# Attention, cosine feed-forward and soft mixture of experts on one core: a weight conversion one tile further ahead, and attention products and a transpose in other slots

## The chip, the core and the metric

One core of one Trainium2 chip runs the kernel. The metric is device time in microseconds (us), the median of three runs. Engines are called as in the profile: PE (matrix products), DVE and POOL (elementwise work), ACT (activations), SP (a queue that issues DMAs).

## The reference

```python
kv = einsum('bhsd,bhse->bhde', k, v);  out = einsum('bhsd,bhde->bhse', q, kv)   # 8 x 8 heads, 576 x 64
x = (out / sqrt(mean(out*out) + 1e-6) * g_norm)        # to 4608 tokens x 512
h = x @ w_in                                           # 512 x 2048
x = (h * cos(h)) @ w_out                               # 2048 x 512
logits = x @ phi                                       # 8 experts x 4 slots
d = softmax of logits over the tokens;  slot_input = d.T @ x
slot_out[e] = relu(slot_input[e] @ w1[e]) @ w2[e]      # 512 x 1024, 1024 x 512
out = (softmax of logits over the slots) @ slot_out
```

## The kernel before, in words

The 4608 tokens are worked in ten blocks j: eight of 512 tokens (0 to 7) and two of 256 (8 and 9, `SMALL` is 8). A block has 16 steps, called slots, one for each 128-column tile f of w_in. In a slot the PE makes `main(j, f)`, 12 products into a PSUM bank called h (L391): w_in is split into a rounded part and a low part, and so is x, and three of the four pairs are multiplied for each of four rows of weights. Then come cos_a (ACT L407 and DVE L410), cos_b (ACT L414) and cos_c (DVE L453, which writes gT and frees the h bank). There are three h banks, so a main can't start until the cos_c of three mains before has run. From block 1's second half on, cos_c is followed by DVE transposes (L460, L472) into `tr`, which DMAs carry to `g`. In blocks 8 and 9 two tiles share one 512-column bank, so that two mains (24 products of 256 columns) go with one cos.

Everything else is put into the slots by tables, and a scheduler isn't used: the order of issue is the order of the code. `at2(j, n, f)` puts a call into slot n of block j, and n of 16 or more means slot n-16 of block j+1. What a slot runs is, from block 2 on: loads, main, side calls (these), cos_a, post, cos_b, cos_c, fin.

For blocks 1 to 9 the attention products of block j's tokens run in block j-1. `att_out(j, t)` makes the products ops for 128 tokens (PE L202), ACT squares them (L211), DVE sums (L213), and POOL raises the sum to the power -0.5 (L216, `ri`). `att_xs` multiplies (DVE L223), `att_xT` transposes on the PE (L241) and copies the rounded part (ACT L245), `att_lo` makes the low part (DVE L254). All of these take a bank of a second ring of four, called at.

The softmax over tokens is a running one. For each block `l_exp` (L573 to L580) makes the exponentials `ld`, `l_T` (PE L594, 64-row transposes `ldT`) turns them to tokens, and DVE copies two halves out of the bank, `d` (L596) and `l_tok` (L604). `slot_acc` (PE L624, `ab`) then adds d.T @ g for the block. The expert stage and the output follow after block 9.

The first 60 us are different. w_in and w_out arrive as 64-bit numbers and are converted in the kernel, tile by tile, in letters of the strings `start`, `one` and `two`: A scales (ACT L301), R shifts (DVE L306), P and L put in the sign and the low bits (DVE L311, L316), H rounds (ACT L322) and S subtracts for the low part (POOL L327). Capital letters are w_in (in `one` and `two` for tile f+2, `LI`), small letters w_out. A token such as A.1 names its tile; m0, f0, r0, b0, c0 are main, the two parts of cos_a, cos_b and cos_c of block 0; s0, p0 and e0 are the side, post and fin calls. Block 1 runs four slots (`L`) behind block 0. `start` also makes block 0's attention; block 1's is in the slots of block 0 that `A[0]` names, one list each for products, multiply, transposes, and low parts.

Of the kernel before, what the change touches and what calls it, by code (L numbers as in the profile page):

```python
# [21 lines left out]
PLAN = dict(  # L22
    ke=(0, 0),
    lp=(0, 0, 0),
    gE=(0, 0),
    co=(3, 4, 4, 5, 6, 7, 7, 8, 9, 10, 10, 11, 12, 12, 13, 13),
    wq=(7, 10, 13, 15),
    l0=(9, 9, 12, 13, 15, 15, 17, 17),
    E=((18, 19, 3, 1), (18, 19, 3, 1)),
    F=((21, 22), (21, 22)),  # L30
    L=4,
    LI=2,
    PI=2,
    start=(
# [3 lines left out]
    ),  # L38
    one='m0 e0 A R f0 P a l0 r0 p0 L r s0 b0 H p c0 S l',
    two='s0 m0 A R m1 a f0 e1 P L l0 f1 r0 r1 s1 l1 p0 r b0 H c0 e0 b1 p c1 l S p1',  # L40
    wm=(3, 5),
    pm=3,
    pa=4,
# [3 lines left out]
    lx=(2, 1),  # L47
    lT=20,
    sa=22,
    A=(((0, 0, 1, 2), (1, 1, 1, 1), (2, 2, 3, 3), (0, 0, 0, 0)),  # L50
       ((9, 10, 11, 12), (0, 0, 0, 0), (11, 12, 13, 14), (0, 0, 0, 0))),
    K=((0, (0, 0, 0, 0)), (1, (1, 3, 5, 7)), (1, (13, 15, 17, 19))),
    KL=(((0, 1), (1, 2), (1, 4), (1, 6)), ((1, 11), (1, 14), (1, 16), (2, 2))),
    ao=(2, 5, 8, 11),
    xs=(1, 1, 1, 1),
    xT=(5, 8, 11, 14),
    lo=(1, 1, 0, 0),
# [7 lines left out]
NB = len(SIZES)  # L65
TT = [n // 128 for n in SIZES]
T0 = [sum(TT[:j]) for j in range(NB)]
NT = sum(TT)
SMALL = SIZES.index(256)
# [3 lines left out]
def tile_linear_attention__ffn_cos__soft_moe(  # L73
# [14 lines left out]
    B, H, D = kv.shape[0], 8, 64  # L88
    NF, KD = w_in.shape[0], w_in.shape[2]
# [31 lines left out]
    sel = const.tile([128, 4, NS], F32, name="sel")  # L121
    A_ = const.tile([128, 576], F32, tag="A", name="A")
    A = A_[:, 0:512]
    m_run = const.tile([128, 1], F32, name="m_run")
# [8 lines left out]
    def at_bank(name):  # L133
        return ps_a.tile([128, 512], F32, tag="at", name=name)
# [5 lines left out]
    q_t, kv_t, vr_t = {}, {}, {}  # L140
    kz = rem_p.tile([128, 2, 512], F32, tag="kr", name="kz")

    def spans(j, t):
        p, r = divmod(T0[j] + t, 9)
        if r == 4:
            return [(0, 64, 2 * p), (64, 64, 2 * p + 1)]
        return [(0, 128, 2 * p + r // 5)]

    def load_q(j, t):
        if j == 0:  # L150
            q_t[j, t] = first["q"][:, t]
        else:
            q_t[j, t] = q_p.tile([128, 4, 128], F32, tag=f"q{(T0[j] + t) % 3}", name="q")
        nc.sync.dma_start(out=q_t[j, t], in_=qT[T0[j] + t])
# [22 lines left out]
    def kv_pair(b, pr):  # L177
        ps = at_bank("kvps")[:, 0:64]
        t = kv_t.pop((b, pr))
        hh = [slice(0, 64), slice(64, 128)]  # L180
        for r in range(4):
            for h in hh:
                nc.tensor.matmul(out=ps[h], lhsT=t[:, 0, r, h], rhs=t[:, 1, r, h], start=(r == 0), stop=False)  # L183
        for h in hh:
            cc = slice(pr * 128 + h.start, pr * 128 + h.stop)
            nc.tensor.matmul(out=ps[h], lhsT=kz[:, b % 2, cc], rhs=vr_t[b // 2][:, cc], start=False, stop=True)
        t = kvbd[b % 2]
        e = PLAN["ke"][b] if b < 2 else 2
        copy_on(e, t[0:64, pr, 0:64], ps[0:64, 0:64])
        copy_on(e, t[64:128, pr, 64:128], ps[64:128, 0:64])  # L190

        kv_done.add((b, pr))
# [4 lines left out]
    def att_out(j, t):  # L197
        ps = at_bank("ops")
        for pr in range(4):
            for p0, n, b in spans(j, t):  # L200
                assert (b, pr) in kv_done
                nc.tensor.matmul(out=ps[p0:p0 + n, pr * 128:(pr + 1) * 128],  # L202
                                 lhsT=q_t[j, t][:, pr, p0:p0 + n], rhs=kvbd[b % 2][:, pr, :],
                                 start=True, stop=True)
        if (j, t) == (1, 2):
            sq = first["wo"][2].rearrange("p (h d) -> p h d", d=D)
        elif j:
            sq = a_p.tile([128, H, D], F32, tag="a", name="sq")
        else:
            sq = first["sx"][:, t].rearrange("p (h d) -> p h d", d=D)  # L210
        nc.scalar.activation(out=sq.rearrange("p h d -> p (h d)"), in_=ps, func=AF.Square)  # L211
        ss = sm_p.tile([128, H], F32, tag="ss", name="ss", bufs=4)
        nc.vector.tensor_reduce(out=ss, in_=sq, axis=AX.X, op=ALU.add)  # L213
        nc.vector.tensor_scalar(out=ss, in0=ss, scalar1=1.0 / D, scalar2=1e-6, op0=ALU.mult, op1=ALU.add)  # L214
        ri = sm_p.tile([128, H, 1], F32, tag="ri", name="ri", bufs=4)
        nc.gpsimd.tensor_tensor(out=ri[:, :, 0], in0=ss, in1=mhalf, op=ALU.pow)  # L216
        o_t[j, t] = (ps, ri, sq)
# [49 lines left out]
    first = {}  # L267
# [621 lines left out]
    def at(j, f, fn, *a):  # L889
        side.setdefault((j, f), []).append((fn, a))  # L890
# [6 lines left out]
    L = PLAN["L"]  # L897
# [6 lines left out]
    def at2(j, f, *a):  # L904
        at(*U(j, f), *a)

    def late2(j, f, *a):
        late(*U(j, f), *a)
# [6 lines left out]
    def end2(j, f, *a):  # L915
        end(*U(j, f), *a)
# [3 lines left out]
    def ld_at(j, f, fn, *a):  # L920
        loads.setdefault(U(j, f), []).append((fn, a))
# [47 lines left out]
            side[NB, 0].insert(0, (exp_table, ()))  # L969

    for j in range(NB):
        lT, sa = (PLAN["F"][j] if j < 2 else (22, 23) if j == NB - 1 else (21, 23) if j == SMALL - 1
                  else (23, 25) if j == SMALL else (PLAN["lT"], PLAN["sa"]))
        at2(j, lT, l_T, j)
        at2(j, sa, slot_acc, j)
        end2(j, sa, slot_add, j)

    for b in range(1, B):
        p, i = divmod(b, 2)
# [3 lines left out]
        for pr in range(4):  # L983
            at2(n, sl[pr], kv_pair, b, pr)

    for j in range(1, NB):
        n = min(j - 1, SMALL - 1)
        ao, dx, xt, dl = PLAN["ao"], PLAN["xs"], PLAN["xT"], PLAN["lo"]
        if n < 2:
            ao, dx, xt, dl = PLAN["A"][n]  # L990
        elif j > SMALL:
            ao, dx, xt, dl = (x[2:] for x in (ao, dx, xt, dl))
        for t in range(TT[j]):
            i = T0[j] + t + 3
            if i < NT:
                jj = max(x for x in range(NB) if T0[x] <= i)
                ld_at(n, ao[t] + 1 + (n > 1), load_q, jj, i - T0[jj])
            at2(n, ao[t], att_out, j, t)
            late2(n, ao[t] + dx[t], att_xs, j, t)
            at2(n, xt[t], att_xT, j, t)  # L1000
            at2(n, xt[t] + dl[t], att_lo, j, t)
# [22 lines left out]
    for u in range(NF):  # L1024
        n, i = 3 + u // 4, u % 4
        a, f = PLAN["nt"][i]
# [52 lines left out]
    steps = dict(A=cv_scale, R=cv_rest, P=cv_top, L=cv_low, H=cv_hi, S=cv_lo)  # L1079
# [3 lines left out]
    def ck(k, w, out):  # L1083
        need = dict(A="", R="A", P="R", L="P", H="L", S="H")[k]
        assert all((x, w, out) in done for x in need), (k, w, out)
        assert (k, w, out) not in done
        done.add((k, w, out))

    def token(t, f):
        k, *arg = t.split(".")  # L1090
        if k.upper() in steps:
            out = int(k.islower())
            ws = [int(arg[0])] if arg else [w for w in range(NF) if PLAN["co"][w] == f] if out else [f + PLAN["LI"]]
            for w in ws:
                if w < NF and (arg or out or w >= PLAN["PI"]):
                    ck(k.upper(), w, out)
                    steps[k.upper()](w, out)
        elif arg:
            a = int(arg[0])
            dict(kv=lambda: kv_pair(0, a), ao=lambda: att_out(0, a), xs=lambda: att_xs(0, a),  # L1100
                 xT=lambda: att_xT(0, a), lo=lambda: att_lo(0, a), warm=lambda: warm(a),
                 win=lambda: load_win(a), wout=lambda: load_wout(a), lkv=lambda: load_kv(a // 4, a % 4),
                 rem=lambda: load_rem(a) if a == 0 else load_kz(0, 1),
                 q=lambda: [load_q(a, t) for t in range(3 if a else TT[0])])[k]()
        else:
            j = int(k[1])
            f -= L * j
            if 0 <= f < NF:
                dict(m=main, s=lambda j, f: run(side, j, f), f=fr_tt, r=round_off, p=lambda j, f: run(post, j, f),
                     b=cos_b, c=cos_c, e=lambda j, f: run(fin, j, f), l=lambda j, f: run(loads, j, f))[k[0]](j, f)  # L1110

    with tc.manual_schedule():
# [20 lines left out]
            if f > 2:  # L1133
                ld_at(0, min(PLAN["co"][f - 3] + 1, 12), load_wout, f)
        for f in range(NF):
            for t in (PLAN["one"] if f < L else PLAN["two"]).split():
                token(t, f)
        for j, f in [(1, f) for f in range(NF - L, NF)] + [(j, f) for j in range(2, SMALL) for f in range(NF)]:
            run(loads, j, f)
# [105 lines left out]
```

## Time and profile before

| | |
|---|---|
| runs | 673.14, 673.9, 674.0 us; median 673.9 |
| the profiled execution | 674.39 us, of which 672.6 us are the span from first to last instruction |
| granted clock of the PE, mean | 0.991 of full |
| busy | PE 646.0 us, DVE 496.1, ACT 328.1, POOL 208.3 |
| DMA | 135.13 MB, mean 201 GB/s |

The 1.8 us between span and time lie outside of what the trace shows. The PE is busy in 96% of the span, so what matters is where it is not: the first 50 us, a few short waits in the middle and the last 20 us.

### The profile page before, as it was taken

To read this page: it belongs to the slowest core of one execution; us is meant where nothing else is said; L and a number is where in the kernel's file an instruction comes from. 1 tells how busy PE (TensorE), PEld (TensorE's weight loads), DVE (VectorE), ACT (ScalarE), POOL (GpSimd) and SP (SyncE) were. 2 spreads that over 40 slices of the span, in tenths; PEclk is the share of its full clock that TensorE was granted. 3 is DMA by queue.
4 is the path that set the end of the run, shared out by engine and by line. 5 is a ranking of instruction groups with operands and counts; after the bars stand their busy time and mean duration, and the time that the engine had idled before them with its cause. 6 is when DMAs were issued, how large, how long until landed. Compare 5 with 4: busy or idle time off the path is not lost.

```text
span 672.6 us, 12593 instructions
## 1 busy us (share of the span) xinstructions
PE 646.0 (96%) x4639; PEld 474.7 (71%) x4639; DVE 496.1 (74%) x909; ACT 328.1 (49%) x589; POOL 208.3 (31%) x291
## 2 busy tenths in 40 slices
PE   6989999999999999999999999999999999999992
PEld 6767777776667776767677677767677778984451
DVE  3799989966677778877887788787877765546143
ACT  3576767645244454445444554544463453552042
POOL 2451111320363333530643253334526322200000
PEclk9899999999999999999999999999999999999997
DMA  9955564111385636783677287576645369899998
GB/s 328 346 192 188 189 228 149 60 35 63 84 200 141 173 79 187 209 234 118 170 212 209 66 207 208 158 212 148 162 122 118 70 166 315 295 413 408 406 416 353
DMA packets 70589, 135.13 MB, mean 201 GB/s; under 512 B 10752, under 2 KB 39040, under 8 KB 69504
## 3 DMA queue, kind: packets, MB, share of 16 engines
q1 hardware_dynamic: 63360, 119.63, 54.3%
q0 software_dynamic: 7168, 14.69, 9.5%
q8 instruction: 37, 0.61, 0.4%
q14 instruction: 24, 0.20, 0.1%
HBM read 91.29 MB, written 13.63 MB: 156 GB/s over the span
## 4 chain that ended last, share of the span: by engine, by line
PE 76%; DVE 8%; ACT 5%; DMA 5%; SPq 2%; issue 2%; POOL 1%; DVEq 0%; ACTq 0%
PE h L391 46%; PE ab L624 5%; PE ops L202 4%; PE l L525 3%; PE xTps L241 2%; PE eh L780 2%; PE eo L817 2%; DMA g<-tr 2%; PE kvps L183 2%; PE tr L494 2%; DVE gT L453 2%; PE l L534 2%; DVE tmp L410 2%; ACT tmp L414 1%; SPq L513 1%
## 5 line engine op out<-in xcount | busy, mean ns | idle before, releaser
L391 PE MATMUL h<-xt,w 128*128 128x512 f32 (+1 forms) x1920 | 420.8, 374 | 3.6 <-DVE gT L453 1.5
L391 PEld LDWEIGHTS h<-xt,w 128*128 128x128 f32 x1920 | 329.4, 189 | 86.4 <-issue 12.7
L414 ACT ACTIVATE tmp<-tmp,hpi 128x512 f32<-128x512 f32 (+1 forms) x145 | 104.2, 720 | 174.2 <-DVE tmp L410 174.1
L513 POOL DMA_DIRECT2D g<-tr x224 | 123.4, 554 | 102.5 <-DVE tr L472 48.8
L453 DVE TENSOR_TENSOR gT<-tmp,h 128x512 f32<-128x512 f32 x130 | 89.1, 686 | 70.5 <-ACT tmp L414 70.5
L216 POOL TENSOR_TENSOR ri<-ss,mhalf 128x8 f32<-128x8 f32 x36 | 59.5, 1655 | 203.7 <-DVE ss L214 203.5
L410 DVE SCALAR_TENSOR_TENSOR tmp<-h,tmp 128x512 f32<-128x512 f32 (+1 forms) x145 | 97.1, 673 | 18.1 <-ACT tmp L407 17.2
L407 ACT ACTIVATE tmp<-h 128x512 int32<-128x512 f32 (+1 forms) x145 | 85.1, 587 | 46.7 <-PE h L391 46.4
L472 DVE STREAM_TRANSPOSE tr<-gT 128x512 f32<-128x512 f32 x103 | 73.2, 711 | 5.9 <-DMA g<-tr 1.6
L327 POOL TENSOR_TENSOR w<-st_m,w 128x512 fp32r<-128x512 f32 x16 | 21.4, 1335 | 63.8 <-ACT w L322 63.8
L202 PE MATMUL ops<-kvA,q 128*128 128x128 f32 (+1 forms) x320 | 38.6, 278 | 0.1
L245 ACT ACTIVATE xt<-xTps,gn 128x512 fp32r<-128x512 f32 x36 | 24.5, 685 | 25.7 <-PE xTps L241 25.7
L202 PEld LDWEIGHTS ops<-kvA,q 128*128 128x128 f32 (+1 forms) x320 | 34.6, 180 | 3.0 <-issue 2.0
L624 PE MATMUL ab<-g,d 128*32 128x512 f32 x256 | 32.3, 593 | 0.0
L525 PE MATMUL l<-gT,wp 128*32 128x512 f32 (+1 forms) x248 | 30.9, 556 | 0.0
L254 DVE SCALAR_TENSOR_TENSOR xt<-xTps,gn,xt 128x512 fp32r<-128x512 f32 x36 | 26.1, 729 | 4.8 <-ACT xt L245 4.6
L211 ACT ACTIVATE sq<-ops 128x512 f32<-128x512 f32 x31 | 18.5, 596 | 21.7 <-PE ops L202 21.6
L213 DVE TENSOR_REDUCE ss<-sq 128x8 f32<-128x512 f32 x31 | 21.0, 676 | 7.5 <-ACT sq L211 7.2
L183 PEld LDWEIGHTS kvps<-kv 128*64 128x64 f32 x448 | 15.4, 137 | 12.5 <-issue 7.6
L624 PEld LDWEIGHTS ab<-g,d 128*32 128x32 f32 x256 | 9.5, 110 | 19.2 <-issue 16.6
L223 DVE TENSOR_TENSOR sq<-ops,ri 128x512 f32<-128x512 f32 x31 | 20.9, 675 | 1.2 <-POOL ri L216 1.2
L241 PE MATMUL xTps<-ident,sq 128*128 128x128 f32 x124 | 19.0, 276 | 1.8 <-DVE sq L223 1.8
(186 smaller groups left out, 605.3 us busy)
## 6 DMA issues: line engine op xcount, KB each, us to landing
kv<-in_kv SPq DMA_DIRECT2D x28, 512.0 KB, 5.7
g<-tr SPq DMA_DIRECT2D x224, 64.0 KB, 3.7
g<-tr POOLq DMA_DIRECT2D x224, 64.0 KB, 3.8
ew<-in_ew SPq DMA_DIRECT2D x23, 512.0 KB, 8.9
q<-in_qT SPq DMA_DIRECT2D x36, 256.0 KB, 6.0
out<-ot SPq DMA_DIRECT2D x11, 768.0 KB, 7.5
rw<-in_w_in SPq DMA_DIRECT2D x16, 512.0 KB, 4.2
nat<-in_w_out SPq DMA_DIRECT2D x16, 512.0 KB, 3.9
```

What stands on the lines that cost most here:

```text
L202: nc.tensor.matmul(out=ps[p0:p0 + n, pr * 128:(pr + 1) * 128], lhsT=q_t[j, t][:, pr, p0:p0 + n], rhs=kvbd[b % 2][:, pr, :], start=True, st ...
L216: nc.gpsimd.tensor_tensor(out=ri[:, :, 0], in0=ss, in1=mhalf, op=ALU.pow)
L241: nc.tensor.transpose(ps[:, kk * 128:(kk + 1) * 128], xs[:, kk * 128:(kk + 1) * 128], ident)
L391: nc.tensor.matmul(out=ps, lhsT=w[:, a, kk, :], rhs=x[b][:, kk, :], start=(n == 0), stop=(n == 3 * KD - 1))
L407: nc.scalar.activation(out=t.bitcast(I32), in_=ps, func=AF.Copy, bias=0.25, scale=INV_2PI)
L410: nc.vector.scalar_tensor_tensor(out=t, in0=ps, scalar=INV_2PI, in1=t.bitcast(I32), op0=ALU.mult, op1=ALU.subtract)
L414: nc.scalar.activation(out=t, in_=t, func=AF.Sin, bias=hpi, scale=TWO_PI)
L453: nc.vector.tensor_tensor(out=g, in0=fr, in1=h_t.pop((j, f)), op=ALU.mult)
L472: nc.vector.transpose(out=tr_t[j, q][:, :, i, :], in_=gT_t[j, n * q + i].rearrange("p (b t) -> p b t", t=32))
L513: (nc.gpsimd if b % 2 else nc.sync).dma_start(out=dst[32 * b:32 * b + 32, :, x, a:a + n, :].rearrange("p t f i -> p t (f i)"), in_=src[32 ...
L525: nc.tensor.matmul(out=l_t[j][32 * o:32 * o + 32, :], lhsT=wp[:, f, :], rhs=gT_t.pop((j, f)), start=(c == 0), stop=(c == (2 if j == NB - 1 ...
L624: nc.tensor.matmul(out=ps[32 * c:32 * c + 32, :], lhsT=d[:, t, :], rhs=gs[c // 2][t][:, (c % 2) * 512:(c % 2) * 512 + 512], start=(t == 0) ...
```

## The change

It has three parts. In the start, the conversion of w_in's tiles is a step further ahead: A.2 stands in `start`, `turn_on` puts H and S of tile 2 and A of tile 3 into slot 0 of block 0 (ahead of block 1's first products), slot 0 has a string of its own without a w_out step or a w_in S, and in the other slots A serves tile f+3 and stands just before H. With it, block 1's four products move from slots 0, 0, 1, 2 to 0, 0, 1, 1, and the fourth q tile gets a buffer of its own in the start. Second, the second product of each later block moves from slot 5 to slot 4 (`ao`). Third, the transposes of block 7's exponentials (l_T) move from slot 5 to slot 6 of block 8.

```diff
-        "xs.2 L.0 H.0 S.0 xT.2 warm.3 lo.0 xs.3 lo.1 xT.3 lo.2 A.1 lo.3 R.1 P.1 L.1 H.1 S.1 "
+        "xs.2 L.0 H.0 S.0 xT.2 warm.3 lo.0 xs.3 lo.1 xT.3 lo.2 A.1 A.2 lo.3 R.1 P.1 L.1 H.1 S.1 "
...
-    one='m0 e0 A R f0 P a l0 r0 p0 L r s0 b0 H p c0 S l',
-    two='s0 m0 A R m1 a f0 e1 P L l0 f1 r0 r1 s1 l1 p0 r b0 H c0 e0 b1 p c1 l S p1',
+    one0='m0 e0 R f0 P l0 r0 p0 L s0 b0 c0',
+    one='m0 e0 R f0 P a l0 r0 p0 L r s0 b0 A H p c0 S l',
+    two='s0 m0 R m1 a f0 e1 P L l0 f1 r0 r1 s1 l1 p0 r b0 A H c0 e0 b1 p c1 l S p1',
...
-    A=(((0, 0, 1, 2), (1, 1, 1, 1), (2, 2, 3, 3), (0, 0, 0, 0)),
+    A=(((0, 0, 1, 1), (1, 1, 1, 1), (2, 2, 3, 3), (0, 0, 0, 0)),
...
-    ao=(2, 5, 8, 11),
+    ao=(2, 4, 8, 11),
...
+        elif (j, t) == (1, 3):
+            q_t[j, t] = first["wo"][3].rearrange("p (r c) -> p r c", r=4)
...
-        if (j, t) == (1, 2):
-            sq = first["wo"][2].rearrange("p (h d) -> p h d", d=D)
+        if j == 1 and t > 1:
+            sq = first["wo"][4 - t].rearrange("p (h d) -> p h d", d=D)
...
-        lT, sa = (PLAN["F"][j] if j < 2 else (22, 23) if j == NB - 1 else (21, 23) if j == SMALL - 1
+        lT, sa = (PLAN["F"][j] if j < 2 else (22, 23) if j == NB - 1 else (22, 23) if j == SMALL - 1
...
+    def turn_on():
+        for k, w in (("H", 2), ("S", 2), ("A", 3)):
+            ck(k, w, 0)
+            steps[k](w, 0)
+
+    at(0, 0, turn_on)
...
-            if i < NT:
+            if 7 < i < NT:
...
-            ws = [int(arg[0])] if arg else [w for w in range(NF) if PLAN["co"][w] == f] if out else [f + PLAN["LI"]]
+            ws = [int(arg[0])] if arg else [w for w in range(NF) if PLAN["co"][w] == f] if out else [f + PLAN["LI"] + (k == "A")]
...
-                 q=lambda: [load_q(a, t) for t in range(3 if a else TT[0])])[k]()
+                 q=lambda: [load_q(a, t) for t in range(4)])[k]()
...
-            for t in (PLAN["one"] if f < L else PLAN["two"]).split():
+            for t in PLAN["one0" if f == 0 else "one" if f < L else "two"].split():
```

POOL at the start, before: L216 are the powers (the first four are block 0's, the next four block 1's), L327 the S steps of tiles 0, 1, 2, 3 and on.

```order
L216 TENSOR_TENSOR ri<-ss,mhalf 128x8 x4
L327 TENSOR_TENSOR w<-st_m,w 128x512 x2
L216 TENSOR_TENSOR ri<-ss,mhalf 128x8 x2
L327 TENSOR_TENSOR w<-st_m,w 128x512
L216 TENSOR_TENSOR ri<-ss,mhalf 128x8
L327 TENSOR_TENSOR w<-st_m,w 128x512
L216 TENSOR_TENSOR ri<-ss,mhalf 128x8
L327 TENSOR_TENSOR w<-st_m,w 128x512 x11
L216 TENSOR_TENSOR ri<-ss,mhalf 128x8
```

The same place after (line numbers are three higher):

```order
L219 TENSOR_TENSOR ri<-ss,mhalf 128x8 x4
L330 TENSOR_TENSOR w<-st_m,w 128x512 x3
L219 TENSOR_TENSOR ri<-ss,mhalf 128x8 x4
L330 TENSOR_TENSOR w<-st_m,w 128x512 x12
L219 TENSOR_TENSOR ri<-ss,mhalf 128x8
```

S of tile 2 now stands ahead of block 1's four powers, and S of tile 3 behind all four, where it stood behind three.

PE in block 4, slots 3 to 6, before (blocks 3 to 7 read alike): the mains, the transposes ldT of block 3, the products ops of block 5's tokens.

```order
L391 MATMUL h<-xt,w 128x512 x24
L594 MATMUL ldT<-ident,ld 128x64 x4
L391 MATMUL h<-xt,w 128x512 x12
L241 MATMUL xTps<-ident,sq 128x128 x4
L202 MATMUL ops<-kvA,q 128x128 x4
L391 MATMUL h<-xt,w 128x512 x12
```

The same place after:

```order
L394 MATMUL h<-xt,w 128x512 x24
L597 MATMUL ldT<-ident,ld 128x64 x4
L205 MATMUL ops<-kvA,q 128x128 x4
L394 MATMUL h<-xt,w 128x512 x12
L244 MATMUL xTps<-ident,sq 128x128 x4
L394 MATMUL h<-xt,w 128x512 x12
```

The products moved from behind the main of slot 5 to ahead of it.

PE in block 8 around l_T of block 7, before:

```order
L391 MATMUL h<-xt,w 128x256 x36
L594 MATMUL ldT<-ident,ld 128x64 x4
L391 MATMUL h<-xt,w 128x256 x24
L525 MATMUL l<-gT,wp 32x256 x4
L624 MATMUL ab<-g,d 32x512 x16
```

And after:

```order
L394 MATMUL h<-xt,w 128x256 x48
L597 MATMUL ldT<-ident,ld 128x64 x4
L394 MATMUL h<-xt,w 128x256 x12
L528 MATMUL l<-gT,wp 32x256 x4
L627 MATMUL ab<-g,d 32x512 x16
```

The transposes went past one main; slot_acc, which reads d, stayed. DVE at the same place, before, from the last step of block 7's l_exp on:

```order
L580 SCALAR_TENSOR_TENSOR s_run<-s_run,mb,sb 128x1
L453 TENSOR_TENSOR gT<-tmp,h 128x512
L460 STREAM_TRANSPOSE tr<-gT 128x2x8x32
L596 COPY d<-ldT 128x128
L604 COPY l_tok<-ldT 128x128
L410 SCALAR_TENSOR_TENSOR tmp<-h,tmp 128x512
L453 TENSOR_TENSOR gT<-tmp,h 128x512
L460 STREAM_TRANSPOSE tr<-gT 128x2x8x32
```

And after:

```order
L583 SCALAR_TENSOR_TENSOR s_run<-s_run,mb,sb 128x1
L456 TENSOR_TENSOR gT<-tmp,h 128x512
L463 STREAM_TRANSPOSE tr<-gT 128x2x8x32
L413 SCALAR_TENSOR_TENSOR tmp<-h,tmp 128x512
L456 TENSOR_TENSOR gT<-tmp,h 128x512
L463 STREAM_TRANSPOSE tr<-gT 128x2x8x32
L599 COPY d<-ldT 128x128
L607 COPY l_tok<-ldT 128x128
```

The copies of d and l_tok moved behind a whole cosine step, that of tiles 4 and 5.

## Rows read from the trace of the kernel before

**Rows 1.** The page: busy time, share of the span and instructions by engine.

```profile
PE 646.0 (96%) x4639; PEld 474.7 (71%) x4639; DVE 496.1 (74%) x909; ACT 328.1 (49%) x589; POOL 208.3 (31%) x291
```

**Rows 2.** Waits of PE from 66 to 660 us: total us, times, longest.

```profile
PE h L391 <- DVE gT L453: 1.3, 5, 0.3
PE ldT L594 <- DVE s_run L580: 0.8, 1, 0.8
```

**Rows 3.** Timeline of PE, 33 to 50 us: start, length, operation, idle before.

```profile
36.90 2.56 PE L391 MATMUL h<-xt,w 128*128 128x512 f32 x10 [1.03 <-POOL w L327]
...
41.54 2.99 PE L391 MATMUL h<-xt,w 128*128 128x512 f32 x12
...
47.16 0.63 PE L241 MATMUL xTps<-ident,sq 128*128 128x128 f32 x4 [1.75 <-DVE sq L223]
...
47.98 2.31 PE L391 MATMUL h<-xt,w 128*128 128x512 f32 x9
```

**Rows 4.** Timeline of POOL, 26 to 50 us.

```profile
26.93 1.28 POOL L327 TENSOR_TENSOR w<-st_m,w 128x512 fp32r<-128x512 f32 x1 [4.01 <-ACT w L322]
32.37 3.24 POOL L216 TENSOR_TENSOR ri<-ss,mhalf 128x8 f32<-128x8 f32 x2 [4.16 <-DVE ss L214]
...
38.61 1.64 POOL L216 TENSOR_TENSOR ri<-ss,mhalf 128x8 f32<-128x8 f32 x1 [1.76 <-DVE ss L214]
```

**Rows 5.** Windows: length, busy time of each engine, granted clock, DMA share, GB/s.

```profile
18.00:19.00 1.00, 1.00 (x8) 0.86 (x8) 0.97 (x3) 0.45 (x1) 1.00 (x2) 0.89 1.02 410
19.00:22.00 3.00, 2.94 (x14) 2.78 (x14) 2.94 (x5) 1.63 (x3) 1.66 (x2) 0.50 1.03 361
22.00:23.00 1.00, 0.84 (x7) 0.60 (x5) 0.75 (x1) 0.28 (x2) 0.93 (x1) 0.90 1.06 287
...
40.00:60.00 20.00, 18.25 (x101) 15.19 (x98) 19.59 (x34) 15.50 (x29) 7.14 (x6) 1.00 0.33 118
46.00:48.00 2.00, 0.84 (x9) 0.87 (x9) 2.00 (x5) 0.97 (x3) 1.18 (x1) 1.00 0.00 0
```

**Rows 6.** Timeline of DVE, 24 to 36 us.

```profile
27.45 1.05 DVE L306 TENSOR_SCALAR st_m<-st_m 128x512 int32<-128x512 int32 x1 [1.32 <-ACT st_m L301]
...
34.12 0.43 DVE L306 TENSOR_SCALAR st_m<-st_m 128x512 int32<-128x512 int32 x1 [0.21 <-ACT st_m L301]
```

**Rows 7.** Timeline of PE in block 4, 300 to 322 us.

```profile
310.79 3.02 PE L391 MATMUL h<-xt,w 128*128 128x512 f32 x12 [0.25 <-DVE gT L453]
...
314.09 1.06 PE L202 MATMUL ops<-kvA,q 128*128 128x128 f32 x8
```

**Rows 8.** Timeline of PE in block 8, 540 to 560 us.

```profile
549.24 0.43 PE L594 MATMUL ldT<-ident,ld 64*128 64x64 f32 x4 [0.77 <-DVE s_run L580]
549.60 3.13 PE L391 MATMUL h<-xt,w 128*128 128x256 f32 x24
552.65 0.64 PE L525 MATMUL l<-gT,wp 128*32 128x256 f32 x8
553.11 4.00 PE L624 MATMUL ab<-g,d 128*32 128x512 f32 x32
```

**Rows 9.** Timeline of DVE in block 8, 540 to 560 us.

```profile
550.54 0.69 DVE L453 TENSOR_TENSOR gT<-tmp,h 128x512 f32<-128x512 f32 x1 [1.32 <-ACT tmp L414]
551.26 0.71 DVE L460 STREAM_TRANSPOSE tr<-gT 128x512 f32<-128x512 f32 x1
551.90 0.25 DVE L596 COPY d<-ldT 128x128 f32<-128x128 f32 x1
...
552.27 0.67 DVE L410 SCALAR_TENSOR_TENSOR tmp<-h,tmp 128x512 f32<-128x512 f32 x1
553.73 0.69 DVE L453 TENSOR_TENSOR gT<-tmp,h 128x512 f32<-128x512 f32 x1 [0.79 <-ACT tmp L414]
```

**Rows 10.** Timeline of PE, 13 to 24 us.

```profile
17.10 0.63 PE L241 MATMUL xTps<-ident,st_x 128*128 128x128 f32 x4 [2.31 <-DVE st_x L223]
```

**Rows 11.** Waits of the DMA queue of SP, 540 to 660 us: total us, times, longest.

```profile
SPq L684 <- PE ab L624: 9.5, 2, 5.7
```

More of the change, by code (lines that the diff above doesn't have):

```diff
@@ L1092, in token @@
             out = int(k.islower())
-            ws = [int(arg[0])] if arg else [w for w in range(NF) if PLAN["co"][w] == f] if out else [f + PLAN["LI"]]
+            ws = [int(arg[0])] if arg else [w for w in range(NF) if PLAN["co"][w] == f] if out else [f + PLAN["LI"] + (k == "A")]
             for w in ws:
-                if w < NF and (arg or out or w >= PLAN["PI"]):
+                if w < NF:
                     ck(k.upper(), w, out)
```

## The prediction

> **What bounds the kernel.** I read the page first: the PE is busy in 96% of the span [rows 1], so a change helps only where it takes away PE time in which nothing runs, and hurts where it makes some. The waits of the PE say where that is. From 66 to 660 us there is little: five waits of the main for the DVE's gT, 1.3 us together, and one of the ldT transposes for the last step of the exponentials, 0.8 us [rows 2]. Before 66 us I read the timeline, as a wait there may be on a path that another engine sets: the PE stands 1.03 us at 36.90 for a POOL subtract and 1.75 us at 47.16 for a DVE multiply [rows 3]. The window from 40 to 60 us shows what bounds that stage: the DVE is busy for 19.59 of 20 us, the PE for 18.25 [rows 5]. There the PE waits because the DVE is full.
>
> **The start: conversion ahead, products in slots 0, 0, 1, 1.** The wait at 36.90 is for S of tile 2, which stands on POOL behind two powers, 3.24 us from 32.37 [rows 4]. After the change S of tile 2 stands ahead of the four powers, so this wait goes. The wait at 47.16 is for block 1's fourth token group; its product now comes a slot earlier and this wait goes too. But S of tile 3 now waits for all four powers. The third of them starts at 38.61 and takes 1.64 [rows 4], the fourth as much, so S of tile 3 starts at about 38.61 + 3.28 = 41.9 and with its 1.28 ends at 43.2. The main of tile 3, which started at 41.54 [rows 3], could start near 40, but its third product reads that result and stands for some 2.5 us. It ends a microsecond later than before; the 1.75 of the next wait is then saved, and the main that started at 47.98 [rows 3] starts some 0.9 us sooner.
>
> Does the end keep this? The DVE has 0.41 us of idle time left in 40 to 60 us [rows 5], and its work is the same before and after. The h banks come free by the DVE's gT, so the PE can't run away from it. What the start is worth is therefore what the DVE gains. I find 0.28 us of idle that can go. Against it stands POOL: while a subtract ran on POOL from 26.93 for 1.28 us [rows 4], a DVE shift that starts at 27.45 took 1.05 us, and 0.43 us at 34.12 with no subtract beside it [rows 6]. So a subtract that falls on such a step costs the DVE 0.6 us. The S steps of tiles 2 and 3 fall elsewhere now; my estimate is that one more of them meets a shift or an or, +0.5, and the sum for the start is **+0.2 us**. The bounds are -0.5, where no subtract meets the DVE and all of its idle goes, and +0.8, where two meet it. The moved DMA is that of a q tile, ahead of the fourth w_in tile on SP's queue; in 46 to 48 us the queues are empty [rows 5], and the mains that need these tiles come long after.
>
> The row on POOL and DVE has a rule beside it: the Trainium skill, page "SBUF — State Buffer", section "Who interferes with whom", says that the pair of ports shared by the two is locked for a whole instruction, not split. By it, the DVE step would stand until the subtract ends; the row's 1.05 us fits, since it ends at 28.50, a shift's length after the 28.21 of POOL less what overlaps.
>
> **The products of later blocks, slot 5 to slot 4.** In blocks 3 to 7 the main of slot 5 follows the ldT transposes at once and waits 0.25 us for gT, which frees its bank [rows 2, 7]. Now the four product groups, about 0.9 us of a row that lasts 1.06 [rows 7], stand between, and cover the wait. By the row the gain is five times 0.25, 1.25 us. The distance of starts says a bit more: a main behind ldT starts 0.36 us after it without a wait (549.24 to 549.60, [rows 8]), and the waiting one loses the overlap too, which makes about 0.35 each. I take **-1.75 us**, with -1.25 as the other end. A product in the new place needs its q tile a slot sooner; its load moves with it. What follows it is late for nobody: its square, sum and power have slot 5's main to run in, 3.02 us [rows 7], and the multiply comes a slot after them.
>
> **l_T of block 7, slot 5 to slot 6.** This takes one wait and makes another. *Gained:* ldT waited 0.77 us at 549.24 [rows 8] for the exponentials. Now main 6 stands there and needs nothing late: the PE goes on at 548.47. A main of 256 columns takes 1.53 us (half of 552.65 - 549.60, [rows 8]), so main 6 ends at 550.0, ldT at 550.4 (0.36), main 7 at 551.9, and l, 0.46 us (553.11 - 552.65, [rows 8]), at 552.35. *Lost:* the next on PE is ab, which reads d. Before, d's copy ran on the DVE at 551.90, directly behind the transposes of tiles 2 and 3, at 551.26 [rows 9], and was there long before ab's start at 553.11 [rows 8]. Now the DVE has the whole cosine step of tiles 4 and 5 first. It starts at 551.90 in d's place. From the DVE's L410 to its L453 it is 553.73 - 552.27 = 1.46 us [rows 9], most of it a wait for ACT that nothing else on the DVE's queue may use; so gT at 553.36. From there to the transposes 0.72 (551.26 - 550.54), from those to the next 0.64 (551.90 - 551.26), and d's copy 0.25 [rows 9]: d stands at 553.36 + 0.72 + 0.64 + 0.25 = 554.97, and ab starts at 555.0. That is **+1.89 us** against 553.11, the 0.77 already taken off. The PE stands for 555.0 - 552.35 = 2.65 us at one place where it stood 0.77 before. The end can't be under +1.5, since the DVE's chain has no step that can be left out, nor much over 2.1. The queue behind ab on the PE is block 8's next four mains, so all of them are late.
>
> **The clock.** The granted clock of the PE falls once in the middle of work: it was 0.89 from 18 us, 0.50 from 19 to 22 and 0.90 in the next microsecond [rows 5], with the PE busy for nearly all of it. This is half of full speed, 1.2 of 2.4 GHz. It lost 0.11 + 1.5 + 0.1 = 1.7 us of clock. What came before was a stand of 2.31 us, which ended at 17.10 [rows 10]. The stand of 1.75 us that ended at 47.16 was not followed by a fall, 46 to 48 us having 1.00 [rows 3, 5]. The new stand of 2.65 us is longer than the one that the fall followed, so I expect one behind it, at the price of that one: **+1.7 us**, with ab and the mains behind it in the slow stretch. The other end is nothing.
>
> The Trainium skill, page "TensorE: Matmul & The Clock Gate", Part 1, also has two levels, but read strictly it would keep the clock up through a stand of this length; the row at 17.10 speaks against that. By the page the sum would be without these 1.7 us.
>
> **Sum.** 0.2 - 1.75 + 1.89 + 1.7 = +2.04 us. On the profiled execution's 674.39 (672.6 of span and 1.8 around it) this is 676.4; that execution lies 0.5 above the median of 673.9, so on the median's side it is **675.9 us**. The delay at 555 reaches the end: the expert weights' loads that stand ahead of the last stage wait themselves for the PE (9.5 us of SP's queue waits for ab, [rows 11]), and move with it.
>
> **Rivals.** (a) *The clock stays up.* Speaking for it: 1.75 us did no harm, and the PE works without a stop ahead of 548, which it did not at 13 us. Then 673.9 + 0.34 = 674.2. Chance 0.25. (b) *Faster: the start's gain is kept whole.* If the DVE isn't the bound up to 66 us, the stands of 1.03 and 1.75 us that go are worth 2.78 us to the end; without a fall of the clock that gives 673.9 - 2.78 - 1.75 + 1.89 = 671.3. It decides from about 1.5 of the 2.78 us on. Against it speak 19.59 of 20 us on the DVE [rows 5], and S of tile 3 behind four powers. Chance 0.1. (c) *The tail hides it.* If the expert weights' DMAs and not the PE set the last 80 us, gain and loss up to 560 us are both swallowed and the time stays near 673.9. Against it, SP's waits for PE [rows 11]. Chance 0.1. The forecast with the fall of the clock keeps 0.55.
>
> **Numbers.** What a measurement of this kernel tells from no change is about 0.2%, 1.35 us. The likeliest case's own range: the lowest ends are -0.5 - 1.75 + 1.5 and a fall of only the three microseconds at 0.50, +1.5, together +0.75, 674.7; the highest 0.8 - 1.25 + 1.89 + 1.7 = +3.1, 677.0. It is over 675.25 in some 85 of 100 of it. The range over all cases is **672.9 to 677.0**, which leaves out (b) and a little at the top. Slower 0.47 + 0.03 of (a) = 0.50; faster 0.10 of (b) + 0.02 = 0.12; the rest, 0.38, within 0.2%.
>
> **What would show it.** Right: no wait of ldT in block 8 and one of ab for d of 2 to 3 us near 554, a granted clock of 0.5 in the microseconds after; no waits for gT at slot 5 in blocks 3 to 7; at the start no stand at 36.9 and 47.2 but one of some 2 us inside the main of tile 3, and block 1's later mains at their old times near 66 us. Wrong: mains at 100 us more than 1 us sooner (b), a clock of 1.00 near 556 (a), or an end that hasn't moved while ab has (c). I am wrong altogether if d's copy comes before the cosine step.

## The result, and the profile after

The changed kernel takes 677.51 us (median of six runs, 676.43 to 679.26) against 673.95 for the kernel before (six runs). The ratio is 1.0054 with a 95% interval of 1.004 to 1.0069: 2.7 to 4.7 us slower. The direction was forecast, the size was not: 675.9 was predicted, with a range up to 677.0.

The profiled execution took 677.64 us, its span is 675.9, and 3.3 us of difference to the span before have to be found. I set the start of the same step of the PE in both traces side by side. After is 1.0 us ahead at 26 us, level at 48, 0.79 behind at 65 and still at 194, 1.41 behind at 227, 0.14 ahead at 541, 1.75 behind when ab of block 7 starts and 4.07 when it has ended. After that the distance stays, and the last 0.7 us are won back behind the PE's last work. So there are four places.

**Block 8.** The PE's timeline after, from 540 us, answers to [rows 8]:

```profile
543.46 6.31 PE L394 MATMUL h<-xt,w 128*128 128x256 f32 x48
549.70 0.46 PE L597 MATMUL ldT<-ident,ld 64*128 64x64 f32 x4
550.09 1.69 PE L394 MATMUL h<-xt,w 128*128 128x256 f32 x12
551.71 0.64 PE L528 MATMUL l<-gT,wp 128*32 128x256 f32 x8
554.86 6.31 PE L627 MATMUL ab<-g,d 128*32 128x512 f32 x32 [2.51 <-DVE d L599]
561.11 6.01 PE L394 MATMUL h<-xt,w 128*128 128x256 f32 x48
```

The 0.77 us stand of ldT is gone, and ab stands 2.51 us for d. But ab itself also takes 6.25 us to the next main, where it took 557.04 - 553.11 = 3.93. The DVE after, which answers to [rows 9], has d's copy where it was forecast, behind the whole cosine step:

```profile
551.75 0.65 DVE L413 SCALAR_TENSOR_TENSOR tmp<-h,tmp 128x512 f32<-128x512 f32 x1
553.19 0.69 DVE L456 TENSOR_TENSOR gT<-tmp,h 128x512 f32<-128x512 f32 x1 [0.79 <-ACT tmp L417]
553.92 0.71 DVE L463 STREAM_TRANSPOSE tr<-gT 128x512 f32<-128x512 f32 x1
554.55 0.25 DVE L599 COPY d<-ldT 128x128 f32<-128x128 f32 x1
```

**The clock.** Windows after (the third number from the right is the granted clock), which answer to [rows 5]:

```profile
18.00:19.00 1.00, 0.94 (x9) 0.75 (x8) 1.00 (x2) 0.19 (x1) 1.00 (x2) 1.00 1.04 422
19.00:22.00 3.00, 2.31 (x18) 1.81 (x17) 3.00 (x6) 1.89 (x4) 2.24 (x2) 1.00 1.05 369
...
43.00:44.00 1.00, 1.00 (x5) 0.77 (x5) 1.00 (x3) 0.44 (x1) 0.49 (x1) 0.79 0.11 37
44.00:47.00 3.00, 3.00 (x12) 2.51 (x11) 2.31 (x5) 1.17 (x3) 0.79 (x1) 0.50 0.00 0
...
555.00:556.00 1.00, 1.00 (x5) 0.32 (x4) 0.60 (x2) 0.36 (x1) 0.00 (x0) 0.79 1.02 420
556.00:559.00 3.00, 3.00 (x18) 1.76 (x17) 1.40 (x2) 0.36 (x1) 0.00 (x0) 0.50 1.02 438
```

In this execution the stand of 2.31 us before 17 us was followed by no fall, the stand in tile 3's main was, and the one at ab was. In the trace of the kernel before it is the first that fell [rows 5, 10]. Which stand is followed by a fall differs from one execution to the next: of the thirteen traces of this study that have the stand of 2.31 us, eight show a fall behind it, and of the seven that have one of some 1.9 us in tile 3's main, four.

**The start.** PE and POOL after, which answer to [rows 3, 4]:

```profile
42.26 3.53 PE L394 MATMUL h<-xt,w 128*128 128x512 f32 x10 [1.90 <-POOL w L330]
...
47.95 2.31 PE L394 MATMUL h<-xt,w 128*128 128x512 f32 x9
```

```profile
37.74 3.24 POOL L219 TENSOR_TENSOR ri<-ss,mhalf 128x8 f32<-128x8 f32 x2 [2.45 <-DVE ss L217]
40.94 1.27 POOL L330 TENSOR_TENSOR w<-st_m,w 128x512 fp32r<-128x512 f32 x1
```

The two stands went and the one behind four powers came, as forecast, and at 48 us nothing is won. What is lost by 65 us lies on the DVE: two of its steps that a subtract on POOL meets are longer. First the kernel before, DVE and then POOL, then after:

```profile
50.50 1.19 DVE L316 SCALAR_TENSOR_TENSOR st<-st 128x512 int32<-128x512 int32 x1
...
54.37 0.69 DVE L410 SCALAR_TENSOR_TENSOR tmp<-h,tmp 128x512 f32<-128x512 f32 x1 [0.28 <-ACT tmp L407]
...
56.24 1.20 DVE L311 SCALAR_TENSOR_TENSOR st<-st 128x512 int32<-128x512 int32 x1
```

```profile
49.72 1.42 POOL L327 TENSOR_TENSOR w<-st_m,w 128x512 fp32r<-128x512 f32 x1 [2.54 <-ACT w L322]
55.54 1.35 POOL L327 TENSOR_TENSOR w<-st_m,w 128x512 fp32r<-128x512 f32 x1 [4.39 <-ACT w L322]
```

```profile
50.61 1.64 DVE L319 SCALAR_TENSOR_TENSOR st<-st 128x512 int32<-128x512 int32 x1
...
57.03 1.79 DVE L314 SCALAR_TENSOR_TENSOR A<-st,A 128x512 int32<-128x512 int32 x1
```

```profile
50.40 1.30 POOL L330 TENSOR_TENSOR w<-st_m,w 128x512 fp32r<-128x512 f32 x1 [5.61 <-ACT w L325]
56.58 1.69 POOL L330 TENSOR_TENSOR w<-st_m,w 128x512 fp32r<-128x512 f32 x1 [4.87 <-DVE gT L456]
```

Without a subtract beside it such a step takes 0.68 us. In all four pairs the DVE's step ends 0.55 us after POOL's (before: 51.69 and 51.14, 57.44 and 56.89; after: 52.25 and 51.70, 58.82 and 58.27). The subtract starts 0.68 us later at the first place, as H, which it waits for, now stands behind A on ACT. The two steps are 0.45 + 0.59 = 1.04 us longer; less the 0.28 of idle at 54.37 that goes, this is 0.76 of the 0.79 us by which this pair of traces differs at 65 us. A third step behind it is longer as well (1.68 us at 65.07, where it took 1.16). How far one pair of traces can be trusted here is taken up behind the experiments on the start.

**Blocks 3 to 7.** The waits for gT are gone; the products fill the place ([rows 7] before, here block 3):

```profile
249.56 0.46 PE L597 MATMUL ldT<-ident,ld 64*128 64x64 f32 x4
249.94 1.16 PE L205 MATMUL ops<-kvA,q 128*128 128x128 f32 x8
250.86 3.01 PE L394 MATMUL h<-xt,w 128*128 128x512 f32 x12
```

From 1.41 us behind to 0.14 ahead is 1.55 us, 0.31 for each of five blocks. The fourth place, block 2, where 0.6 us are lost between 194 and 227 us, is taken up among the experiments.

### The profile page after: what moved, and what is told of

Read it like the earlier page. It is cut to its first block, busy times and chain, and to the rows that moved or that the text cites. A ratio compares the mean times of both kernels' runs of the same rounds, so it can differ in the third digit from the quotient of the medians.

```text
span 675.9 us, 12582 instructions
## 1 busy us (share of the span) xinstructions
PE 649.2 (96%) x4639; PEld 476.5 (71%) x4639; DVE 495.9 (73%) x909; ACT 328.3 (49%) x589; POOL 209.4 (31%) x291
## 4 chain that ended last, share of the span: by engine, by line
PE 84%; DVE 7%; DMA 2%; ACT 2%; issue 1%; POOL 1%; SPq 0%; DVEq 0%; ACTq 0%
PE h L394 53%; PE ab L627 5%; PE ops L205 4%; PE l L528 4%; PE kvps L186 2%; PE eh L783 2%; PE eo L820 2%; PE xTps L244 2%; PE l L537 2%; PE tr L497 2%; DVE tmp L413 1%; PE lr L553 1%; DMA ew<-in_ew 1%; PE fo L849 1%; DMA kv<-in_kv 1%
## 5 line engine op out<-in xcount | busy, mean ns | idle before, releaser
L627 PE MATMUL ab<-g,d 128*32 128x512 f32 x256 | 34.7, 620 | 2.8 <-DVE d L599 2.5
L627 PEld LDWEIGHTS ab<-g,d 128*32 128x32 f32 x256 | 11.1, 114 | 23.0 <-issue 18.5
L216 DVE TENSOR_REDUCE ss<-sq 128x8 f32<-128x512 f32 x30 | 20.4, 678 | 9.1 <-ACT sq L214 8.9
L186 PE MATMUL kvps<-kv 128*64 128x64 f32 x448 | 18.3, 226 | 1.4 <-DMA kv<-in_kv 1.4
```

Source lines behind the costliest of these rows:

```text
L627: nc.tensor.matmul(out=ps[32 * c:32 * c + 32, :], lhsT=d[:, t, :], rhs=gs[c // 2][t][:, (c % 2) * 512:(c % 2) * 512 + 512], start=(t == 0) ...
```

## The experiments

Medians over up to 12 runs are given with the difference to the kernel before on the same chip, and the 95% interval of the ratio. The kernel before itself spread from 672.6 to 677.5 us in the first group, so a difference under about 1 us isn't certain.

**One part at a time.** l_T alone, on the kernel before:

```diff
-        lT, sa = (... else (21, 23) if j == SMALL - 1
+        lT, sa = (... else (22, 23) if j == SMALL - 1
```

> The kernel before with l_T of block 7 alone moved to slot 6. Theory (the transposes' move makes ab wait for d, and the clock falls behind that stand): +1.89 us of stand, as forecast, and +2.3 us of clock, as the profile after shows (ab 4.00 to 6.31 us), so +4.2 us, 678.1; with the clock at the forecast 1.7, +3.6. Rival (the clock falls only in the profiled execution): +1.9 us, 675.9. Rival (the loss is in the start): no more than +0.5.

Measured 677.38 us, +3.2 (1.003 to 1.006). This is nearly the whole loss. Its trace has the stand, but no fall behind it, and ab still takes 560.30 - 555.43 = 4.87 us:

```profile
555.43 4.93 PE L624 MATMUL ab<-g,d 128*32 128x512 f32 x32 [2.51 <-DVE d L596]
560.30 6.01 PE L391 MATMUL h<-xt,w 128*128 128x256 f32 x48
```

```profile
556.00:559.00 3.00, 3.00 (x29) 1.07 (x27) 1.57 (x3) 0.72 (x1) 0.00 (x0) 1.00 1.02 437
```

So 0.94 us of ab's growth is not the clock, and the forecast had no term for it; the clock's share where it falls is 6.25 - 4.87 = 1.4. In the other executions of l_T alone there can't be many such falls: the mean granted clock of its twelve runs is 0.9903, the same as that of the 35 runs of the kernel before beside them, and a fall of 1.7 us behind each stand would take 0.0025 off. In this pair of traces l_T costs 3.24 us at the end of block 8 less 0.44 that it was behind at 543 us: 2.8 us, 1.89 + 0.94.

The other two parts without l_T (its line undone in the changed kernel):

> The changed kernel with l_T of block 7 back in slot 5: the start and the products in slot 4 alone. Theory (start +0.8 by 65 us and +0.6 in block 2, products -1.55): 673.95 - 0.15 = 673.8. By the forecast's own terms (+0.2, -1.75): 672.4. Rival (the stand of 0.6 us in block 2's ab is chance): 673.2.

674.46 us, +0.3 (0.9987 to 1.0017). The PE is 0.80 us behind at 160 us and 1.30 at 239, and 0.13 at 543: the start's loss and the products' gain cancel.

The products alone (`ao=(2, 4, 8, 11)` on the kernel before):

> The kernel before with the second product of blocks 3 to 8 alone moved to slot 4. Theory: five times 0.31 us, -1.55, 672.4, and no wait for gT behind ldT. Rival (the wait only moves to a later main, or the tail is bound by DMA): within 0.3 us of before.

673.39 us, -0.75 (0.9975 to 1.0011, so not told from no change). In the trace the mains of 240 to 540 us wait for nothing, and the PE gains 1.4 us from 239 to 543; the end keeps it there (span 670.5).

The start alone:

> The start's part alone (conversion a tile ahead, block 1's products in slots 0, 0, 1, 1). By the profile after: +0.8 us at 65 us and, if the stand in block 2's ab belongs to it, +1.4: 674.7 to 675.3. The forecast's term: +0.2, 674.1. Rival (the removed stands come through): -1 or more.

675.94 us, +1.8 (1.0006 to 1.0038): a loss where the forecast had +0.2. The trace has 1.40 us by 160 us and 0.8 more in block 2, 0.6 of it a wait of ab for a transfer of g.

**The stand at ab.** slot_acc of block 7 two slots later in the changed kernel, `(22, 25)`:

> The changed kernel with slot_acc of block 7 two slots later, behind the mains of tiles 8 and 9. Theory (all of the loss at 555 us is the wait of ab for d and what hangs on it): the two mains, 3.05 us, cover the 2.5 us stand; no fall of the clock there, and ab's sixteenths come at their old pitch; ldT's wait of 0.77 us stays away too. That leaves the start and the products, about +0.3, less 0.77: 673.5. Rival (the expert weights' loads wait for ab, and a later ab holds up the tail): the loss comes back in the tail, 675 to 677. Rival (the loss isn't from d's wait): 677.5 as before.

675.63 us, +1.5 (0.9998 to 1.0034), 1.9 under the changed kernel but 2 over what was expected. The trace agrees with the theory at its place in part: no stand, no fall, and from 543 to 580 us it is 0.06 us faster than before. But ab isn't at its old pitch, as was expected: it takes 560.16 - 555.78 = 4.38 us instead of 3.93. The rest of what the trace misses is lost ahead of this place: it was 2.06 us behind at 239, 0.8 of which is again a wait for g in block 2.

23 warming products in the stand (`at2(j, sa, warm, 23)` ahead of slot_acc):

> The changed kernel with 23 warming products of 128 columns (some 2.4 us, no part of the computation's output) put into the stand ahead of ab of block 7. They keep the PE busy and leave d where it is. Theory (the clock falls behind this stand in some executions, at 1.4 us, and the other 0.9 us of ab's length come from the semaphore steps that the PE's queue now runs between the first products): no fall at 555 us in the profile, ab 4.9 us long instead of 6.3, time 0.5 to 1.4 us under the changed kernel's, 676.1 to 677. Rival (the whole of ab's 2.3 us is the clock): 675.2. Rival (the clock has no part): 677.5.

678.08 us, +4.0 (1.004 to 1.0079), slower than each theory: the 23 took 5.4 us, not 2.4, and ab began 2.7 us later. This miss was useful, since ab then took only 561.17 - 557.60 = 3.57 us:

```profile
552.27 5.40 PE L752 MATMUL warm<-ident 128*128 128x128 f32 x46
557.60 3.64 PE L627 MATMUL ab<-g,d 128*32 128x512 f32 x32
```

Eleven of them:

> The changed kernel with 11 warming products in the stand ahead of ab of block 7; the 23 of the run before took 5.4 us, so that 11 fill 2.6. Theory: ab starts at its old place in the changed kernel (within 0.3 us), no fall of the clock, and the semaphore steps run ahead under the warming products, so ab takes 3.6 us and not 6.3 or 4.9; against the changed kernel -2.3 where its clock falls and -1.3 where it doesn't: 675.3 to 676.2. Rival (the loss is the stand alone): 677.5.

677.41 us, +3.1 (1.0037 to 1.0067), the number of the rival. No fall behind 555 us, ab begins at 555.07, but takes 4.77 us: I was wrong that the semaphore steps run ahead under the warming products. They stand in the PE's queue behind the wait for d, whatever the PE does meanwhile. Times of these 16 steps (the first few come before d is asked for; PEldq is the queue of the PE's weight loads) in the trace of the kernel before, of the single move, with 23 and with 11 warming products:

```profile
L624 PEldq EVENT_SEMAPHORE  x16: 51/51/51, 551.4 to 553.4; - x16
```

```profile
L624 PEldq EVENT_SEMAPHORE  x16: 51/51/51, 551.7 to 556.7; - x16
```

```profile
L627 PEldq EVENT_SEMAPHORE  x16: 51/51/51, 555.5 to 557.2; - x16
```

```profile
L627 PEldq EVENT_SEMAPHORE  x16: 51/51/51, 553.0 to 556.2; - x16
```

Where the last step ends ahead of ab's first product (557.2 against 557.60), ab takes 3.57 us; where it comes 1.1 or 1.3 us behind it, ab takes 4.77 and 4.87. The kernel before had its last step at 553.4, 0.3 behind 553.11, and 3.93. The run with slot_acc two slots later in the changed kernel lies between, with its last step at 556.5, 0.7 behind 555.78, and 4.38. In the six traces where d is ready less than 1 us ahead of ab, the last step starts 1.2 to 1.3 us after the end of d's copy (in the single move 556.7 against 555.38), which fits steps that wait behind d. That the steps are what lengthens ab is the reading that fits all these traces; no run takes the steps away.

slot_acc late on the kernel before (`(21, 25)`, l_T in its old slot):

> The kernel before with nothing but slot_acc of block 7 two slots later (l_T in its old slot). It tells why the two runs with a late slot_acc gained less in their medians than in their traces. Theory 1 (a later ab holds up the loads that wait for it, in most executions): 1 to 2 us slower than before, 675 to 676, and the wait stands in the last 100 us. Theory 2 (chance, or the start): the same as before, 674.1, ab being only moved.

674.23 us, -0.1 (0.999 to 1.0014): a late slot_acc holds up nothing, theory 2. Its trace has no part of the change in the start and still waits for g in block 2, by 1.1 us:

```profile
PE ab L624 <- DMA g<-tr: 1.1, 1, 1.1
```

So the waits for g in block 2, 0.6 to 1.1 us in five traces of this study, need no part of the change; they come and go with the execution (whether the start makes them more frequent can't be told from single traces), and the 0.6 us between 194 and 227 us in the profile after are at that place too (shown there as a gap that waits for nothing seen).

**The start's parts.** Products of block 1 back in slots 0, 0, 1, 2, conversion ahead as in the change:

> The start's part alone with block 1's four products back in slots 0, 0, 1, 2; the conversion stays a tile ahead. Theory (the start's loss is that A stands before H and so S meets DVE steps later): S still starts late, the loss stays within 0.5 us of the start alone, 675.5 to 676. Rival (the loss comes of S of tile 3 behind four powers and the 1.9 us stand in its main): the stand is 0.4 us or gone, and the time near 674.2.

676.5 us, +2.15 (1.002 to 1.0047). The stand for POOL is down to 0.5 us and the loss is not smaller, so the rival is refuted as it was put: four powers ahead of S of tile 3 aren't needed for the loss. But a stand is still there. It is now at block 1's fourth token group, longer than the 1.75 us before, and in this trace the clock falls behind it (0.50 from 47 to 50 us):

```profile
46.41 0.71 PE L244 MATMUL xTps<-ident,st 128*128 128x128 f32 x4 [2.17 <-DVE st L226]
```

A behind H again, so that H and with it S come sooner:

```diff
-    one='m0 e0 R f0 P a l0 r0 p0 L r s0 b0 A H p c0 S l',
+    one='m0 e0 R f0 P a l0 r0 p0 L r s0 b0 H A p c0 S l',
```

(`two` likewise.)

> The start's part alone with A behind H again in the strings (b0 H A p c0 S l, and the like in the other), so that S of each tile, which waits for H, starts on POOL 0.6 to 0.7 us sooner. Theory (the start's loss is DVE time lost to POOL's subtracts: the DVE step ends 0.55 us after the subtract, 0.45, 0.59 and 0.52 us more at three places than before): that loss goes, about -1 us against the start alone, near 673.9 to 674.9. Rival (the loss is the 1.9 us stand in tile 3's main, or the clock behind it): no change against the start alone, 675.9.

675.17 us, +1.1 (0.9999 to 1.0025), 0.8 under the start alone. This is about what was expected, but the two intervals overlap, so that the medians don't show a gain. Its two steps on the DVE end 0.55 us after POOL's as well (51.60 and 51.05, 58.37 and 57.82), and the second is shorter:

```profile
49.82 1.78 DVE L314 SCALAR_TENSOR_TENSOR st<-st 128x512 int32<-128x512 int32 x1
...
56.97 1.40 DVE L314 SCALAR_TENSOR_TENSOR st<-st 128x512 int32<-128x512 int32 x1
```

```profile
49.75 1.30 POOL L330 TENSOR_TENSOR w<-st_m,w 128x512 fp32r<-128x512 f32 x1 [3.71 <-ACT w L325]
56.54 1.28 POOL L330 TENSOR_TENSOR w<-st_m,w 128x512 fp32r<-128x512 f32 x1 [5.49 <-ACT w L325]
```

They are 0.59 + 0.20 = 0.79 us longer than before, where the change has 1.04; the PE is 0.94 behind at 160 us, no less than in the profile after. That A ahead of H makes the loss is therefore argued and not shown.

**What the start costs.** One pair of traces isn't enough to tell, since the clock falls at different places in them: at 18.8 us before and at 43.6 after. The table sets all traces side by side by these falls. Its time runs from block 0's first transposes (17.10 us before) to the third step of the DVE that writes gT (63.67 before). The two runs with a piece of the start's part undone are left out, and one of the two in the second row has the nine warming products of the last run below.

| falls of the clock from 16 to 50 us | without the start's part | with it |
|---|---|---|
| one, at 17 to 19 us | 46.3 to 46.6 us (4 traces) | 47.4 (2) |
| none | 45.8 (2) | none seen |
| one, behind the stand in tile 3's main | none seen | 47.6 to 48.1 (3) |
| both | none seen | 48.4 (1) |

So the start's part costs 1.0 us at the same fall, and 2.0 where its own new stand is followed by a fall too (48.4 against 46.4, 47.8 against 45.8). Of the first, 0.6 lies in the two steps that meet a subtract (1.51 + 1.78 us in one of the two traces, against 1.19 + 1.20, less the 0.28 of idle); the second shows on the DVE, which in these four traces waits 0.5 to 1.1 us for ACT at 46 to 47 us and in the other two doesn't:

```profile
46.46 0.69 DVE L413 SCALAR_TENSOR_TENSOR tmp<-h,tmp 128x512 f32<-128x512 f32 x1 [0.66 <-ACT tmp L410]
```

The run with A behind H has a fall at 18 us only and takes 47.6 us, no less than the two beside it.

**Versions that might beat both.** The products in slot 4, l_T in slot 6 and slot_acc in slot 9, with no part of the start:

> The kernel before with the products in slot 4, l_T of block 7 in slot 6, and slot_acc of block 7 in slot 9; no part of the start. Theory: -1.5 of the products and -0.8 of ldT's wait, with no stand at ab: 671.8. Rival (the tail hides it, or a later ab holds up the loads): 673 or more.

673.89 us, -0.2 (0.998 to 1.0013): the rival's number. The traced execution took 671.23, the shortest of the twelve, and its granted clock didn't fall before 661 us; the others took 672.66 to 676.2.

The products, and nine warming products in the stand at 17 us:

> The kernel before with the products of the later blocks in slot 4 and nine warming products in the stand of 2.3 us before block 0's first transposes (no part of the computation's output). Theory (products -1.5; the clock falls behind that stand in most executions, and costs what the traces with and without the fall differ by at 160 us, 0.6 to 1): 671.8, and no granted clock under 1 before 60 us. Rival (up to 66 us the DVE sets the time, so that the fall costs nothing): 672.5 to 673.4, as with the products alone.

674.34 us, no change (0.999 to 1.0016), slower than theory and rival had it. The clock stays at 1.00 in the start, and the PE is 0.59 us ahead at 160 us, where the run of the products alone was 0.41 ahead with a fall. By the table above the fall itself costs about 0.6 us (46.4 against 45.8), less than the 1.7 of clock that it takes; but the nine products also start the transposes later, at 17.25 instead of 16.87, so that little is left. No version clearly beats the kernel before.

## Why the prediction was wrong

**l_T, the stand: right.** +1.89 us were forecast at ab's start and 1.75 + 0.14 = 1.89 measured, with d's copy where the chain of DVE steps put it.

**The clock: a term too much for l_T.** A fall behind the stand was forecast at 1.7 us, as the likeliest case; it came in the changed kernel's trace at 1.4. In the trace of l_T alone it didn't come, and over its twelve runs the mean clock is that of the kernel before. So the condition of rival (a), a clock that stays up, held there, and its price was still too low, by the next term.

**A term was missing in l_T.** ab's own length was taken as unchanged. The semaphore steps for g, most of which used to pass before ab's first product, now come behind the wait for d: +0.94 us. Stand and steps make 2.83; l_T alone measured 3.2 in the medians (2.0 to 4.0). That l_T's sum (1.89 + 1.7) came near this is luck: 0.94 was left out, and 1.7 put in that the runs of l_T alone don't show.

**The start: the step that failed.** "One more of them meets a shift or an or, +0.5" was a guess about where the subtracts fall. No more of them met (five in either trace up to 66 us); those that met did so later, and cost the DVE 0.45 and 0.59 us more. That they were later because A had gone ahead of H on ACT is read from the queue's order; the run made to show it doesn't decide it. The pair of traces says +0.79 where +0.2 was forecast, and the start alone +1.8 in the medians (0.4 to 2.6), over the upper end of 0.8. The table above gives +1.0 for traces with the same fall of the clock, and +2.0 where the new stand in tile 3's main is followed by one. For that stand the forecast had a length, some 2.5 us, and no clock, though it expected a fall at ab because 2.65 us is longer than 2.31; by the same argument 2.5 is too. That no gain of the two stands would last, the ground on which the forecast stood, was right: in the three traces with that stand and no fall behind it the main that started at 47.98 starts 0.7 to 0.9 us sooner, as forecast, and at 65 us they are 0.6 to 0.9 behind.

**The products: right in the traces, too large.** 1.75 us forecast, 1.55 and 1.4 in two traces; the median of the part alone, -0.75 (-1.7 to +0.7), doesn't contradict these but doesn't show a gain either.

Of 3.56 us in the medians, l_T brings about 3.2 (all but the 0.3 of the changed kernel without l_T, and as much as l_T alone), and the start and the products together 0.3, where their terms gave -1.55. That is where the forecast missed: the start alone lies 1.6 above its term and the products alone 1.0, each uncertain by about 1 us. Rival (b) is refuted by the start alone, rival (c) by a PE that keeps its 4 us to the end. The start alone, 1.8 us slower in the medians, lies between the 1.0 and 2.0 of the table. What stays open: why the clock falls behind a stand in one execution and not in the next, and whether another order of A and H would take away the start's 1.0 us.

## What to carry to other kernels

Before a step is moved past another on one engine, follow it to the engine that waits for its result, and write down the order of the queue there: the transposes were moved past one main on the PE, and their copy went past a whole cosine step on the DVE. When a product that waits for many things gets a late first condition, the waits behind it in the queue can become visible too (0.94 us here). Before a stand is explained from one pair of traces, look at where the clock fell in each. Where an engine is full, count what a move does to its collisions with a neighbour from rows, with start and end of both, not as a share of cases.

## What was not expected of the hardware

ab's length follows the time of its last semaphore step: 3.57 us where that step is ahead of the first product, and 3.93, 4.38, 4.77 and 4.87 where it is 0.3, 0.7, 1.1 and 1.3 us behind. The PE doesn't stand idle in the profile's sense; its products only come slower.

POOL's subtract can be the longer one too: it took 1.69 us instead of 1.30 where it started while a DVE step was running (56.58). A warming product of 128 columns in 32-bit floats is two instructions in the trace and takes 0.23 us (23 in 5.4 us). And the clock fell in one trace behind a stand of 1.90 us, while another of 2.51 us was not followed by a fall.
